# One attention-and-MLP kernel, four tables: another order, other engines for evictions and masks, other PSUM banks and turns

## The chip, the cores and the metric

The kernel runs on one core of a Trainium2 chip. The metric is the time of one execution on the device in microseconds (us); less is better. TensorE is called PE, VectorE DVE, ScalarE ACT, GpSimd POOL, and SP is the engine whose queue issues all DMAs.

## The reference, cut to what matters

```
x = A_x                                        # 1 x 2048 x 512, bf16
x = x + A(layernorm(x), A_wqkv, A_wo)          # twice, with the same weights:
x = x + B(layernorm(x), B_w1, B_b1, B_w2, B_b2)
x = x + A(layernorm(x), ...);  x = x + B(layernorm(x), ...)

def A(x, wqkv, wo):                            # 32 heads of 16, window of 256
    q, k, v = split(x @ wqkv)
    scores = q k^T * 16 ** -0.5, kept where 0 <= i - j < 256
    return (softmax(scores) v) @ wo
def B(x, w1, b1, w2, b2):                      # 512 -> 1792 -> 512
    return gelu(x @ w1 + b1) @ w2 + b2
```

## The kernel before

The 2048 rows are 16 tiles of 128, and the two repetitions give 32 tile numbers (0 to 31). Attention works on 16 blocks of two tiles. For a block, layernorm runs on DVE (statistics, L618 and L620) and POOL (the power -0.5, L630); the normalized tile xn (L640) is transposed by a DMA into xnTA (L645; the first four tiles by PE); PE makes Q and K (8 matmuls of 256 columns for two of four chunks, L666) and V (4 matmuls of 512 per tile), which ACT or DVE evict from PSUM (L609 on ACT, L607 on DVE, K always on DVE at L700). V is copied by two DMAs to Vs, shifted by half a tile (L715).

The scores come in *visits*: a block has 10 of them, numbered from 0 (block 0 and block 8, which begin a repetition, have 5). A visit is 8, 12 or 24 small matmuls of 32 rows (L767) into four PSUM banks, then two exps of 128x1024 on ACT (L774), each of which frees two banks, then one or two masks that multiply E (L795, on DVE or POOL). Two *P times V steps* per block (L819, 128 small matmuls, 64 in blocks 0 and 8) need all visits of their half; DVE and POOL transpose and normalize the result (L828, L832, L836, L842), and four matmuls per tile with Wo and a residual addition (L868) end the attention.

The MLP runs in ten jobs (0 to 9) of 2 or 4 tiles: xnTB by DMA transpose, 14 chunks of W1 (4 matmuls each, of 512 or 256 columns), gelu on ACT (6 chunks get their bias on DVE first, L891; ACT loads another table whenever it turns from exp to gelu or back), then per tile 14 matmuls with W2 and an addition on DVE (L911). W1 and W2 are both W_sb in the profile; W2's rows have gT beside it, W1's xnTB. 18 dummy matmuls (L559) on zeros fill PE where nothing else is there.

The program first builds a list of 3078 nodes, in the order of the algorithm. Every engine runs its own queue in order. What stands where is set by tables of numbers that were written beforehand: `_ORDER`, the order of all nodes, from which each engine's queue follows; `_ALT`, the nodes that run on their second engine (ACT instead of DVE for an eviction, POOL instead of DVE for a mask or a normalization, DVE instead of POOL for an epsilon addition); `_BANKS`, the PSUM bank of each allocation in that order, of eight; `_TURNS`, pairs of nodes of which the second waits for the first although it needs nothing of it. `_Plan.run` applies them, and `_Sched.op` puts in a semaphore wait wherever a node depends on another engine's node:

```
for i in _ALT:
    nodes[i]["eng"], nodes[i]["fn"] = nodes[i]["alts"][1]
for a, z in zip(_TURNS[0::2], _TURNS[1::2]):
    nodes[a]["writes"] = nodes[a]["writes"] + ["turn%d" % z]
    nodes[z]["reads"] = nodes[z]["reads"] + ["turn%d" % z]
    nodes[z]["deps"].add(a)
```

Of the kernel before, what the change touches and what calls it, by code (L numbers as in the profile page):

```python
# [19 lines left out]
class _Sched:  # L20
# [147 lines left out]
    3, 14, 4, 0, 16, 33, 1, 18, 2, 34, 20, 37, 24, 32, 56, 36, 17, 35, 57, 25, 58, 60, 19, 61, 41, 59, 22, 62, 106,  # L168
    46, 63, 30, 64, 39, 67, 65, 27, 104, 40, 68, 66, 21, 107, 29, 38, 105, 69, 15, 108, 23, 109, 49, 80, 81, 82, 54,
    113, 70, 83, 110, 114, 55, 5, 111, 6, 71, 115, 72, 112, 73, 84, 116, 13, 126, 74, 117, 42, 118, 47, 119, 152, 194,  # L170
    120, 7, 127, 48, 150, 128, 195, 129, 131, 153, 97, 151, 130, 154, 98, 196, 99, 155, 100, 85, 86, 8, 324, 101, 366,
    9, 87, 156, 368, 88, 158, 75, 103, 76, 521, 10, 90, 91, 367, 11, 102, 92, 89, 93, 12, 77, 197, 78, 94, 198, 322,
    132, 200, 133, 369, 134, 79, 143, 144, 157, 135, 199, 202, 145, 96, 146, 204, 136, 201, 95, 147, 137, 138, 139,
    325, 323, 203, 216, 140, 121, 159, 122, 326, 123, 217, 205, 124, 327, 26, 141, 125, 218, 212, 328, 207, 330, 214,
    522, 160, 206, 208, 161, 162, 163, 213, 329, 170, 43, 370, 209, 164, 171, 210, 372, 148, 172, 173, 175, 149, 176,
    174, 31, 371, 215, 374, 177, 178, 376, 211, 331, 165, 219, 166, 167, 44, 519, 168, 375, 379, 179, 142, 381, 220,
    45, 378, 520, 169, 373, 180, 380, 181, 182, 221, 183, 384, 184, 383, 337, 386, 338, 222, 339, 382, 340, 185, 223,
    385, 394, 28, 377, 224, 395, 225, 341, 226, 230, 231, 388, 396, 232, 233, 387, 398, 234, 227, 397, 400, 228, 389,
    229, 399, 306, 237, 402, 235, 187, 403, 188, 238, 332, 236, 390, 189, 239, 190, 240, 404, 347, 348, 349, 241, 350,
    191, 243, 407, 351, 523, 342, 408, 524, 343, 344, 345, 242, 401, 333, 409, 346, 412, 334, 335, 244, 414, 352, 353,  # L180
    525, 354, 50, 527, 355, 413, 359, 336, 411, 360, 51, 361, 362, 391, 192, 356, 405, 563, 415, 252, 565, 253, 259,
    416, 260, 357, 262, 254, 263, 363, 193, 261, 281, 255, 564, 410, 256, 248, 392, 249, 257, 282, 528, 245, 250, 246,
    266, 269, 247, 270, 267, 406, 526, 284, 258, 264, 285, 641, 52, 283, 417, 271, 393, 53, 268, 265, 186, 272, 418,
    273, 286, 278, 251, 279, 287, 275, 274, 276, 639, 280, 288, 544, 419, 545, 289, 546, 420, 422, 277, 567, 547, 556,
    421, 557, 307, 308, 640, 558, 642, 568, 548, 423, 643, 559, 644, 424, 425, 560, 309, 310, 645, 569, 427, 647, 428,
    311, 426, 290, 312, 313, 571, 432, 646, 314, 566, 573, 315, 433, 562, 316, 317, 318, 319, 572, 570, 320, 576, 648,
    321, 429, 577, 430, 534, 574, 539, 431, 540, 541, 578, 581, 434, 535, 542, 582, 579, 435, 529, 896, 530, 536, 537,
    543, 583, 649, 436, 650, 651, 437, 652, 538, 591, 653, 438, 531, 532, 584, 659, 593, 291, 580, 549, 533, 550, 551,
    592, 552, 440, 292, 293, 553, 294, 595, 585, 660, 597, 661, 441, 575, 295, 898, 662, 586, 596, 439, 358, 599, 587,
    296, 554, 600, 297, 298, 299, 561, 300, 301, 601, 588, 604, 663, 365, 589, 302, 303, 605, 304, 449, 487, 456, 305,  # L190
    457, 606, 897, 609, 458, 450, 611, 654, 607, 655, 590, 442, 656, 610, 657, 899, 452, 451, 453, 658, 443, 475, 613,
    463, 454, 464, 459, 444, 460, 476, 469, 461, 455, 470, 900, 484, 594, 472, 465, 901, 445, 471, 446, 466, 477, 603,
    467, 447, 462, 478, 473, 902, 479, 468, 485, 602, 664, 474, 612, 665, 480, 481, 608, 482, 486, 598, 666, 903, 448,
    904, 683, 667, 483, 503, 614, 905, 488, 364, 615, 489, 684, 490, 491, 555, 492, 685, 687, 616, 668, 493, 617, 494,
    688, 495, 496, 497, 498, 689, 686, 691, 618, 499, 500, 693, 501, 624, 625, 502, 626, 627, 692, 696, 628, 669, 670,
    698, 671, 695, 631, 672, 916, 690, 917, 697, 632, 673, 701, 918, 919, 702, 619, 699, 620, 920, 621, 703, 711, 700,
    622, 504, 505, 623, 713, 704, 506, 507, 508, 629, 509, 712, 715, 510, 630, 511, 1016, 633, 716, 676, 634, 677,
    1018, 678, 679, 717, 719, 705, 512, 637, 513, 514, 694, 721, 515, 714, 706, 1019, 1017, 718, 720, 680, 1020, 638,
    1021, 724, 707, 723, 516, 681, 726, 517, 921, 722, 922, 675, 923, 708, 924, 725, 518, 729, 925, 933, 730, 934,
    935, 936, 731, 727, 906, 728, 940, 1024, 907, 941, 908, 733, 909, 732, 942, 709, 734, 710, 937, 910, 1022, 944,  # L200
    735, 943, 926, 946, 927, 928, 929, 911, 945, 1023, 736, 912, 948, 737, 930, 947, 738, 1025, 913, 949, 914, 739,
    939, 740, 915, 741, 742, 950, 635, 953, 743, 744, 745, 955, 951, 746, 749, 747, 636, 954, 748, 958, 952, 1036,
    1037, 751, 1038, 959, 1039, 750, 752, 1040, 753, 960, 968, 754, 969, 757, 1026, 1027, 962, 1028, 1029, 957, 970,
    755, 972, 1030, 758, 974, 956, 976, 961, 977, 756, 963, 971, 674, 973, 682, 964, 978, 981, 932, 975, 982, 786,
    965, 787, 979, 1273, 788, 789, 983, 986, 1274, 790, 781, 980, 782, 988, 770, 985, 771, 772, 773, 987, 984, 1060,
    783, 784, 1061, 764, 989, 765, 775, 785, 776, 990, 1062, 777, 766, 774, 778, 1064, 779, 767, 966, 1066, 991, 768,
    1065, 1068, 992, 792, 1070, 793, 794, 795, 812, 1063, 1069, 827, 993, 828, 967, 829, 830, 802, 1072, 1275, 803,
    813, 814, 832, 815, 1276, 797, 798, 796, 822, 817, 1277, 831, 818, 1278, 799, 800, 780, 1031, 823, 1279, 996,
    1032, 994, 997, 801, 824, 825, 816, 759, 819, 1280, 1281, 820, 791, 760, 995, 848, 804, 805, 761, 821, 998, 807,
    808, 826, 1067, 762, 809, 864, 810, 806, 763, 999, 1001, 811, 1002, 1000, 1003, 1071, 1004, 769, 1033, 1034, 1005,  # L210
    1073, 833, 1006, 834, 835, 1008, 836, 837, 838, 1007, 839, 1009, 1074, 840, 1010, 1035, 849, 1011, 850, 851, 1075,
    852, 1014, 1078, 853, 1080, 854, 1076, 855, 1395, 856, 1077, 857, 858, 1079, 1088, 1012, 841, 842, 1089, 1081,
    859, 860, 861, 1082, 843, 1090, 1013, 844, 845, 846, 862, 847, 1092, 1015, 1041, 1093, 1042, 863, 880, 1043, 931,
    1044, 1083, 1094, 938, 1045, 1096, 1282, 1084, 881, 1097, 882, 883, 884, 865, 1396, 866, 1393, 1098, 867, 1101,
    1394, 1095, 868, 1103, 869, 1397, 1099, 870, 871, 1091, 872, 1398, 873, 1102, 1106, 885, 1399, 886, 1108, 1085,
    887, 888, 1086, 889, 890, 1107, 1317, 1100, 1104, 874, 875, 1319, 891, 1109, 892, 893, 894, 1318, 1321, 895, 876,
    877, 1105, 878, 1087, 1322, 1298, 1299, 1110, 879, 1300, 1301, 1323, 1293, 1294, 1302, 1295, 1296, 1325, 1324,
    1297, 1111, 1327, 1326, 1330, 1112, 1332, 1329, 1288, 1331, 1113, 1335, 1401, 1114, 1289, 1290, 1337, 1291, 1121,
    1328, 1115, 1122, 1336, 1345, 1292, 1123, 1124, 1320, 1116, 1347, 1117, 1334, 1125, 1118, 1338, 1119, 1346, 1349,
    1128, 1283, 1284, 1120, 1285, 1350, 1286, 1333, 1129, 1303, 1126, 1304, 1351, 1353, 1127, 1305, 1287, 1130, 1306,  # L220
    1131, 1354, 1339, 1046, 1047, 1048, 1134, 1049, 1355, 1352, 1358, 1132, 1050, 1360, 1340, 1357, 1135, 1307, 1356,
    1359, 1363, 1341, 1133, 1310, 1364, 1361, 1311, 1051, 1312, 1053, 1054, 1365, 1342, 1437, 1362, 1348, 1055, 1056,
    1439, 1313, 1366, 1136, 1137, 1367, 1057, 1314, 1368, 1343, 1438, 1400, 1650, 1441, 1440, 1369, 1402, 1138, 1442,
    1139, 1158, 1058, 1159, 1160, 1140, 1161, 1443, 1059, 1445, 1162, 1141, 1052, 1142, 1447, 1444, 1143, 1344, 1144,
# [758 lines left out]
```

## Time and profile before

| | |
|---|---|
| median of 3 runs | 439.81 us (438.87 to 440.06) |
| the profiled execution | 440.44 us; its span from first to last instruction 438.9 us |
| TensorE's granted clock | 0.998 of full speed |
| busy: PE, ACT, DVE, POOL | 412.5, 386.6, 335.6, 209.1 us |
| DMA | 23.51 MB, 161 DMAs issued by SP |

In the rows of the profile an engine's busy time is the union of its instructions, so matmuls that overlap count once. A row of the timeline merges neighbours of one kind: where it starts, how long it lasts, what it is, how many, and in brackets how long the engine idled ahead of it and what ended that.

### The profile page before, as it was taken

What the parts mean: (1) busy time and instruction counts of PE and PEld (TensorE: products, weight loads), DVE (VectorE), ACT (ScalarE), POOL (GpSimd) and SP (SyncE); (2) the same over time, 40 slices, a digit from 0 to 9 for tenths busy, and PEclk for the clock granted to TensorE, in tenths of its full rate; (3) what the DMA queues carried; (4) which work ended last, traced back from release to release, by engine and by line L of the source; (5) the groups of instructions that cost most, each with busy time, mean ns of one, the idle gap of its engine ahead of it and who ended that gap; (6) DMA issues with size and microseconds to landing.
All of it is one profiled execution on the core that took longest, in us unless ns stands there. A gap on an engine that the chain in (4) does not pass through costs nothing.

```text
span 438.9 us, 16863 instructions
## 1 busy us (share of the span) xinstructions
PE 412.5 (94%) x7497; PEld 227.9 (52%) x7571; DVE 335.6 (76%) x635; ACT 386.6 (88%) x458; POOL 209.1 (48%) x233
## 2 busy tenths in 40 slices
PE   8989999998699988999999999999999999999995
PEld 4555756554444544454454455454564554444662
DVE  6999878689867788976899687878877586655841
ACT  3999988999999899999999999999889989899442
POOL 4675263372555366731566344442443645635140
PEclk9999999999999999999999999999999999999999
DMA  7782812102300303212040111201322013003030
GB/s 234 216 210 39 221 32 52 38 21 40 58 3 13 52 4 46 32 34 44 10 94 2 25 27 28 52 1 33 43 55 50 1 31 82 7 0 76 3 108 25
DMA packets 49060, 23.51 MB, mean 54 GB/s; under 512 B 34268, under 2 KB 48988, under 8 KB 48988
## 3 DMA queue, kind: packets, MB, share of 16 engines
q1 hardware_dynamic: 48988, 22.43, 23.2%
q8 instruction: 60, 0.98, 1.0%
q14 instruction: 12, 0.10, 0.1%
HBM read 8.00 MB, written 2.10 MB: 23 GB/s over the span
## 4 chain that ended last, share of the span: by engine, by line
PE 76%; ACT 10%; DVE 6%; DMA 3%; issue 3%; POOL 1%; SPq 1%; POOLq 0%; DVEq 0%
PE ps L666 59%; ACT E L774 9%; PE ps L767 9%; PE ps L819 7%; DVE OD L828 1%; DVE KT L700 1%; POOL E L795 1%; DMA xnTA<-xn 1%; DMA xnTB<-xn 1%; DVE X L911 1%; DVE stat L618 1%; SPq L645 1%; ACT Va L609 0%; DMA X<-in_A_x_dram 0%; DVE E L795 0%
## 5 line engine op out<-in xcount | busy, mean ns | idle before, releaser
L774 ACT ACTIVATE E<-ps 128x1024 bf16<-128x1024 f32 x300 | 284.0, 1038 | 21.7 <-PE ps L767 20.2
L795 POOL TENSOR_TENSOR E<-E,mask 128x512 bf16<-128x512 bf16 (+2 forms) x112 | 121.6, 1097 | 107.7 <-ACT E L774 43.8
L666 PE MATMUL ps<-W_sb,gT 128*128 128x512 bf16 x415 | 106.5, 380 | 3.2 <-issue 2.5
L666 PE MATMUL ps<-xnTB,W_sb 128*128 128x512 bf16 (+1 forms) x542 | 105.5, 335 | 3.6 <-issue 1.6
L666 PEld LDWEIGHTS ps<-xnTB,W_sb 128*128 128x128 bf16 x560 | 52.0, 98 | 43.9 <-issue 4.3
L666 PE MATMUL ps<-xnTA,Wqkv_sb 128*128 128x256 bf16 x512 | 70.6, 273 | 2.2 <-DVE OD L828 1.1
L767 PE MATMUL ps<-QT,KT 32*128 32x128 bf16 (+3 forms) x1920 | 60.6, 231 | 4.9 <-ACT E L774 2.0
L795 DVE TENSOR_TENSOR E<-E,mask 128x512 bf16<-128x512 bf16 (+2 forms) x124 | 51.2, 438 | 14.1 <-ACT E L774 6.8
L666 PEld LDWEIGHTS ps<-W_sb,gT 128*128 128x128 bf16 x448 | 39.4, 98 | 43.1 <-issue 3.4
L828 DVE STREAM_TRANSPOSE OD<-ps 128x1024 f32<-128x1024 f32 x32 | 40.0, 1249 | 23.7 <-PE ps L819 23.5
L666 PEld LDWEIGHTS ps<-xnTA,Wqkv_sb 128*128 128x128 bf16 x512 | 46.3, 98 | 22.5 <-issue 3.2
L767 PEld LDWEIGHTS ps<-QT,KT 32*128 32x128 bf16 x1920 | 28.5, 92 | 51.3 <-ACT E L774 31.0
L899 ACT ACTIVATE gT<-ps,b1T 128x512 bf16<-128x512 f32 (+1 forms) x80 | 43.7, 606 | 10.1 <-PE ps L666 10.0
L907 POOL TENSOR_TENSOR Xb<-X,b2all 128x512 f32<-128x512 bf16 x32 | 36.8, 1152 | 20.4 <-DVE X L911 11.5
L618 DVE BATCH_NORM_STATS2 stat<-X 128x6 f32<-128x512 bf16 x64 | 43.3, 684 | 2.5 <-DMA X<-in_A_x_dram 1.7
L819 PE MATMUL ps<-E,Va 64*17 64x192 bf16 (+3 forms) x1920 | 39.9, 230 | 3.0 <-ACT E L774 1.3
L700 DVE TENSOR_TENSOR KT<-ps,parmask 128x1024 bf16<-128x1024 f32 x32 | 38.6, 1211 | 5.3 <-PE ps L666 5.1
L891 DVE TENSOR_SCALAR gT<-ps,b1T 128x512 bf16<-128x512 f32 (+1 forms) x60 | 36.8, 631 | 6.3 <-PE ps L666 5.9
L836 POOL TENSOR_TENSOR Nb<-OD,Rc 128x512 bf16<-128x512 f32 x18 | 19.0, 1056 | 42.9 <-DVE Rc L832 28.6
L819 PE MATMUL ps<-E,Vs 64*17 64x128 bf16 (+3 forms) x1920 | 39.2, 230 | 0.0
L630 POOL TENSOR_TENSOR rstd<-rstd,mhalf 128x2 f32<-128x2 f32 (+1 forms) x33 | 24.3, 736 | 28.9 <-DVE rstd L624 27.2
L911 DVE TENSOR_TENSOR X<-Xb,ps 128x512 bf16<-128x512 f32 x32 | 21.6, 682 | 19.2 <-PE ps L666 19.0
(49 smaller groups left out, 362.3 us busy)
## 6 DMA issues: line engine op xcount, KB each, us to landing
Vs<-Va SPq DMA_DIRECT2D x64, 68.0 KB, 2.9
W_sb<-in_B_w_dram SPq DMA_DIRECT2D x4, 512.0 KB, 4.6
out_dram<-X SPq DMA_DIRECT2D x16, 128.0 KB, 2.0
X<-in_A_x_dram SPq DMA_DIRECT2D x3, 512.0 KB, 6.6
Wqkv_sb<-in_A_wqkv_dram SPq DMA_DIRECT2D x4, 256.0 KB, 7.3
W_sb<-in_B_w_dram SPq DMA_DIRECT2D x1, 768.0 KB
W_sb<-in_B_w_dram SPq DMA_DIRECT2D x2, 384.0 KB, 5.2
Wqkv_sb<-in_A_wqkv_dram SPq DMA_DIRECT2D x1, 512.0 KB, 6.9
```

What stands on the lines that cost most here:

```text
L618: add("dve", lambda e, B, t=t, k6=k6: e.bn_stats(stat6[:, k6, :], X[:, t, :]), reads=["X%d" % t], writes=["st%d" % k6], key="bs%d" % (k + j))
L666: r = e.matmul(ps[:, B[g][0], cols], lhsT, rhs, start=st, stop=sp)
L700: add("dve", lambda e, B, g=g, i=i: e.tensor_tensor(out=KT[:, kb, 2 * i : 2 * i + 2].rearrange("p c m a q -> p a (c m) q"), in0=ps[:, B[g] ...
L767: x = e.matmul(ps[:, bk[r], o : o + n], KT[rows, kb, c, m].rearrange("p a q -> p (a q)"), QT[rows, c, q : q + n], start=True, stop=True)
L774: add("act", lambda e, B, g_=g_, gi=gi: e.activation(E[:, 2 * gi : 2 * gi + 2, e0 : e0 + 512], ps[:, B[g_][0] : B[g_][0] + 2, :], AF.Exp, ...
L795: fn = lambda e, B: e.tensor_tensor(out=Ew, in0=Ew, in1=Mw, op=ALU.mult)
L819: x = e.matmul(ps[32 * r : 32 * r + VW, B[g][par], c % 2 * 2 * P + lo : c % 2 * 2 * P + hi], V[rows, (2 * b + m // 2) % VR, c * HC + 2 * r ...
L828: add("dve", lambda e, B: e.transpose(OD[:, s].rearrange("p a c q -> p (a c q)"), ps[:, B[g][0] : B[g][0] + 2, :]), reads=["ps:" + g], wri ...
L891: add("dve", lambda e, B, g=g, fc=fc: e.tensor_scalar(out=gT[:, fc, c0 : c0 + M], in0=ps[:, B[g][0], 0:M], scalar1=b1T[:, fc : fc + 1], sc ...
L899: add("act", lambda e, B, g=g, fc=fc: e.activation(gT[:, fc, c0 : c0 + M], ps[:, B[g][0], 0:M], AF.Gelu_apprx_tanh, bias=b1T[:, fc : fc + ...
L907: add("pool", lambda e, B, t=t, xs=xs: e.tensor_tensor(out=Xb[:, xs, :], in0=X[:, t, :], in1=b2all[:], op=ALU.add), reads=["X%d" % t, "b2a ...
L911: add("dve", lambda e, B, g=g, t=t, xs=xs: e.tensor_tensor(out=X[:, t, :], in0=Xb[:, xs, :], in1=ps[:, B[g][0], :], op=ALU.add), reads=["X ...
```

## The change

The four tables are replaced; no line of the program besides them differs, and the 3078 nodes are the same. The tables' numbers tell a reader nothing, so the first lines of two stand for them. The new tables are two lines shorter, so line 666 before is line 664 after.

```
 _ORDER = [
-    3, 14, 4, 0, 16, 33, 1, 18, 2, 34, 20, 37, 24, 32, 56, 36, 17, 35, 57, 25, 58, 60, 19, 61, 41, 59, 22, 62, 106,
...
 _ALT = [
-    62, 66, 69, 74, 94, 101, 108, 115, 120, 184, 191, 197, 201, 206, 210, 215, 219, 356, 363, 369, 373, 377, 378, 383,
...
```

ACT has 440 nodes before and 435 after, DVE 635 and 647, POOL 229 and 222; PE keeps 1613 and SP 161. `_ALT` names 171 nodes before and 163 after, `_TURNS` has 182 pairs before and 166 after. A node's place in PE's queue moves by 10.5 places on average, at most 94.

Three places show what moves. The first is on PE, in attention block 4, from its visit 3 to its visit 7. L767 rows are visits (QT and KT are Q and K transposed), the others what PE does between them. Before:

```order
L767 MATMUL ps<-QT,KT 128x192 x8
L767 MATMUL ps<-QT,KT 128x128 x4
L666 MATMUL ps<-Wo_sb,OT 128x512 x4
L767 MATMUL ps<-QT,KT 128x128 x8
L767 MATMUL ps<-QT,KT 128x64 x16
L666 MATMUL ps<-xnTA,Wqkv_sb 128x256 x8
L767 MATMUL ps<-QT,KT 128x256 x8
L666 MATMUL ps<-xnTA,Wqkv_sb 128x256 x8
L767 MATMUL ps<-QT,KT 128x256 x8
L767 MATMUL ps<-QT,KT 128x192 x8
L767 MATMUL ps<-QT,KT 128x128 x4
```

and after, where L767 has become L765:

```order
L765 MATMUL ps<-QT,KT 128x192 x8
L765 MATMUL ps<-QT,KT 128x128 x4
L664 MATMUL ps<-Wo_sb,OT 128x512 x5
L765 MATMUL ps<-QT,KT 128x128 x8
L765 MATMUL ps<-QT,KT 128x64 x16
L664 MATMUL ps<-Wo_sb,OT 128x512 x3
L664 MATMUL ps<-Wqkv_sb,xnTA 128x512 x4
L765 MATMUL ps<-QT,KT 128x256 x8
L664 MATMUL ps<-xnTA,Wqkv_sb 128x256 x8
L765 MATMUL ps<-QT,KT 128x256 x8
L765 MATMUL ps<-QT,KT 128x192 x8
L765 MATMUL ps<-QT,KT 128x128 x4
```

The last two rows of each piece are visit 7. Before, the gaps hold four matmuls with Wo, eight for K and eight for Q, and nothing ahead of visit 7; after, eight with Wo, four for V and eight for K, and again nothing ahead of visit 7.

The second place is on PE in block 6, from visit 3 on. The piece of before ends with visit 6, the one of after just ahead of it. Before:

```order
L767 MATMUL ps<-QT,KT 128x192 x8
L767 MATMUL ps<-QT,KT 128x128 x4
L666 MATMUL ps<-xnTA,Wqkv_sb 128x256 x2
L767 MATMUL ps<-QT,KT 128x128 x8
L767 MATMUL ps<-QT,KT 128x64 x16
L666 MATMUL ps<-xnTA,Wqkv_sb 128x256 x6
L666 MATMUL ps<-Wo_sb,OT 128x512 x2
L767 MATMUL ps<-QT,KT 128x256 x8
L666 MATMUL ps<-Wo_sb,OT 128x512 x6
L767 MATMUL ps<-QT,KT 128x256 x8
```

and after:

```order
L765 MATMUL ps<-QT,KT 128x192 x8
L765 MATMUL ps<-QT,KT 128x128 x4
L664 MATMUL ps<-xnTA,Wqkv_sb 128x256 x8
L664 MATMUL ps<-W_sb,gT 128x512 x4
L765 MATMUL ps<-QT,KT 128x128 x8
L765 MATMUL ps<-QT,KT 128x64 x16
L664 MATMUL ps<-W_sb,gT 128x512
L664 MATMUL ps<-Wo_sb,OT 128x512 x4
L664 MATMUL ps<-W_sb,gT 128x512
L765 MATMUL ps<-QT,KT 128x256 x8
L664 MATMUL ps<-W_sb,gT 128x512 x2
L664 MATMUL ps<-Wo_sb,OT 128x512 x4
```

The W_sb,gT rows are tile 7's matmuls with W2. Before, all of them are done ahead of visit 1 of this block; after, eight of the fourteen stand in these gaps, and Q's eight are no longer split by a visit.

The third place is SP's queue, near the start. Before, from the load of Wo to the DMA transpose of tile 7 (the last row):

```order
L586 DMA Wo_sb<-in_A_wo_dram 128x4x512
L715 DMA Vs<-Va 64x544 x2
L645 DMA_TRANSPOSE xnTA<-xn 128x4x128
L715 DMA Vs<-Va 64x544 x2
L645 DMA_TRANSPOSE xnTA<-xn 128x4x128
L715 DMA Vs<-Va 64x544
L645 DMA_TRANSPOSE xnTA<-xn 128x4x128
L588 DMA W_sb<-in_B_w_dram 128x4x768
L715 DMA Vs<-Va 64x544 x2
L645 DMA_TRANSPOSE xnTA<-xn 128x4x128
```

and after, from a load of W2 (128x4x512 at L595) to the first transposes into xnTB; tile 7's transpose is the second of the pair ahead of Wo:

```order
L595 DMA W_sb<-in_B_w_dram 128x4x512
L713 DMA Vs<-Va 64x544 x2
L586 DMA W_sb<-in_B_w_dram 128x4x512
L643 DMA_TRANSPOSE xnTA<-xn 128x4x128 x2
L584 DMA Wo_sb<-in_A_wo_dram 128x4x512
L565 DMA X<-in_A_x_dram 128x4x512
L713 DMA Vs<-Va 64x544 x2
L595 DMA W_sb<-in_B_w_dram 128x4x512
L643 DMA_TRANSPOSE xnTB<-xn 128x4x128 x2
```

Wo is loaded behind tile 7's transpose, where it was loaded ahead of all transposes. The two loads of W2's first eight chunks (the first row of this piece and the one ahead of xnTB) stood before next to each other, behind the first two transposes into xnTB.

At the program's end, PE's queue after has job 9's 56 matmuls with W1 in one piece, then tile 31's 14 with W2, then tile 30's 14; before, the matmuls of both tiles are mixed with each other and with job 9's.

394 rows, old and new, of tables (_ALT, _BANKS, _ORDER, _TURNS) are left out of this document.

## The prediction

> **What bounds the kernel now.** I read the page's engine shares and chain first, then the busy time by stretches of 20 us, then the timeline where TensorE falls short. The page:
>
> ```profile
> PE 412.5 (94%) x7497; PEld 227.9 (52%) x7571; DVE 335.6 (76%) x635; ACT 386.6 (88%) x458; POOL 209.1 (48%) x233
> PE 76%; ACT 10%; DVE 6%; DMA 3%; issue 3%; POOL 1%; SPq 1%; POOLq 0%; DVEq 0%
> ```
>
> TensorE (PE) is the bound: 412.5 of 438.9 us busy and 76% of the chain. ScalarE (ACT) is close behind with 386.6. The change gives PE no less to do, so only PE's idle time, 26 us, can be won or lost. The stretches say where it lies (span, then busy time of PE, weight loads, DVE, ACT, POOL, granted clock):
>
> ```profile
> 20.00:40.00 20.00, 17.58 (x446) 11.31 (x444) 18.89 (x33) 18.91 (x22) 15.16 (x18) 1.00 0.55 132
> 40.00:60.00 20.00, 18.87 (x298) 12.02 (x300) 15.92 (x32) 18.30 (x27) 8.10 (x10) 1.00 0.68 152
> 80.00:100.00 20.00, 18.80 (x447) 9.76 (x450) 16.25 (x30) 19.46 (x23) 11.04 (x13) 1.00 0.16 33
> 100.00:120.00 20.00, 15.06 (x434) 8.75 (x434) 17.62 (x34) 19.59 (x23) 8.67 (x10) 1.00 0.31 53
> 160.00:180.00 20.00, 17.97 (x438) 9.12 (x443) 18.24 (x36) 18.94 (x22) 11.69 (x13) 1.00 0.34 43
> 240.00:260.00 20.00, 19.73 (x378) 9.96 (x383) 14.95 (x30) 19.52 (x24) 8.22 (x11) 1.00 0.14 28
> 340.00:360.00 20.00, 19.53 (x416) 10.74 (x419) 13.65 (x24) 18.27 (x23) 9.97 (x11) 1.00 0.04 9
> ```
>
> From 240 us on PE idles 0.3 to 0.5 us in 20: nothing is to be won there, only lost. Before 180 us it loses 2.4, 1.1, 1.2, 4.9 and 2.0 us in the five stretches shown. In the worst one, 100 to 120 us, ACT is busy 19.59 of 20: there PE waits for ACT.
>
> **The prices.** Timeline rows of PE (start, length, line, operation, count; L666 are full-width matmuls, L767 a visit of scores, L819 the P times V step):
>
> ```profile
> 97.34 0.40 PE L767 MATMUL ps<-QT,KT 32*128 32x192 bf16 x12
> 98.12 1.04 PE L666 MATMUL ps<-xnTA,Wqkv_sb 128*128 128x256 bf16 x8
> 99.09 0.41 PE L767 MATMUL ps<-QT,KT 32*128 32x128 bf16 x24
> 118.69 0.81 PE L666 MATMUL ps<-xnTB,W_sb 128*128 128x512 bf16 x3 [0.82 <-ACT E L774]
> 119.43 0.70 PE L767 MATMUL ps<-QT,KT 32*128 32x128 bf16 x24
> 121.46 0.40 PE L767 MATMUL ps<-QT,KT 32*128 32x256 bf16 x8
> 121.79 1.90 PE L666 MATMUL ps<-xnTB,W_sb 128*128 128x512 bf16 x8
> 124.66 0.24 PE L819 MATMUL ps<-E,Va 64*17 64x64 bf16 x8
> 125.90 0.40 PE L767 MATMUL ps<-QT,KT 32*128 32x192 bf16 x12
> ```
>
> A 512-column matmul costs (1.90 - 0.81) / 5 = 0.218 us, I take 0.216. A visit costs 121.79 - 121.46 = 0.33. Three matmuls from 118.69 end their issue at 119.34 and the visit starts at 119.43: a change from full-width work to a visit costs 0.10. Eight 256-column matmuls take 99.09 - 98.12 - 0.10 = 0.87, so 0.11 each. A P times V step costs 125.90 - 124.66 = 1.24. For ACT (a row of the chain, and two rows of groups):
>
> ```profile
> 107.22 12.94 ACT E L774 x14
> L609 ACT ACTIVATE Va<-ps 128x512 bf16<-128x512 f32 x17 | 10.5, 615 | 0.8 <-PE ps L666 0.8
> L607 DVE CAST Va<-ps 128x512 bf16<-128x512 f32 x15 | 10.2, 687 | 1.6 <-PE ps L666 1.3
> ```
>
> One exp costs 12.94 / 14 = 0.924 us, an eviction 0.6. A visit feeds two exps (1.85 us of ACT) and takes 0.43 of PE: PE needs 1.42 us of other work, some 6.5 matmuls of 512 columns, between two visits, or it runs ahead of ACT until the PSUM banks are full, and waits.
>
> **The change, part by part.** PE gets the same instructions, ACT the same exps and gelus and as many table loads, so nothing is removed. Five evictions go from ACT to DVE: 5 x 0.615 = 3.1 us less on ACT and 5 x 0.687 = 3.4 us more on DVE, which has 103 us free. Of 236 masks, 56 go from POOL to DVE and 54 the other way. The rest is order.
>
> *First stage, blocks 3 to 5 (97 to 121 us).* I count the order. From visit 8 of block 3 (97.34) to visit 0 of block 5 (121.46) before issues 12 visits, 28 matmuls of 512 and 40 of 256 columns, 2 P times V steps and 10 changes: 3.96 + 6.05 + 4.40 + 2.48 + 1.00 = 17.9 us. ACT gets 24 exps and 3 evictions: 22.2 + 1.8 = 24.0. The stage took 24.1: ACT's time, and PE lost 6.2. After puts 38 instead of 28 matmuls of 512 columns there, 20.0 us (the first order excerpt shows three gaps between visits of it: 4 and 16, then 12 and 8 matmuls of 512 and 256 columns). But an excess of ACT's work over PE's can also build up over a longer piece: the worst one that I find runs from visit 1 of block 3 to visit 9 of block 4, with 36 exps and 2 evictions (34.5 us) against 18 visits, 60 and 52 matmuls, 3 steps and 15 changes (29.8 us): 4.7. The loss goes from 6.2 to 4.7, **1.5 us gained**. Bounds: 0, if ACT comes to the stage with more left to do than before; 2.8, if only the first piece counts (24 exps and 2 evictions, 23.4, against 20.0: 3.4 left of 6.2).
>
> *Second stage, blocks 6 and 7 (157 to 172 us).*
>
> ```profile
> 157.20 0.40 PE L767 MATMUL ps<-QT,KT 32*128 32x192 bf16 x12
> 172.06 0.40 PE L767 MATMUL ps<-QT,KT 32*128 32x256 bf16 x8 [0.15 <-ACT E L774]
> 173.58 0.60 PE L666 MATMUL ps<-xnTB,W_sb 128*128 128x512 bf16 x2 [0.36 <-DMA xnTB<-xn]
> 169.36 4.17 DMA xnTB<-xn
> ```
>
> Before has 21 matmuls of 512 and 16 of 256 columns, 8 visits, 2 steps, 6 changes there: 4.5 + 1.8 + 2.6 + 2.5 + 0.6 = 12.0 us; it took 14.9, so PE lost 2.9. ACT's 16 exps and an eviction are 15.4. After holds back eight matmuls of tile 7's W2 step for this place (the second order excerpt), and the largest excess I count in blocks 6 and 7 is 1.1 us (visit 9 to visit 1: 4 exps, 3.7, against 2 visits, 8 matmuls and 2 changes, 2.6). **1.8 gained**, bounds 0 (the wait only moves) and 2.9 (none is left). The wait for the transpose into xnTB that follows (0.36) I leave as it is: on SP the same two transposes stand before that job.
>
> *The SP queue.* Rows of the chain, of SP, of the DMA groups and of PE:
>
> ```profile
> 47.91 4.19 DMA xnTA<-xn
> 26.15 1.21 SPq L645 DMA_TRANSPOSE xnTA<-xn  x1
> Wo_sb<-in_A_wo_dram SPq DMA_DIRECT2D x1, 512.0 KB, 7.4
> W_sb<-in_B_w_dram SPq DMA_DIRECT2D x4, 512.0 KB, 4.6
> 32.93 1.25 PE L666 MATMUL ps<-Wo_sb,OT 128*128 128x512 bf16 x5 [0.20 <-ACT E L774]
> ```
>
> Near 48 us a transpose into xnTA is in flight for 4.19 us behind two weight loads, and the chain runs through it. After issues the two 512 KB loads of W2 ahead of the xnTB transposes that SP waits for (third excerpt), so only the two smaller ones still stand around the xnTA transposes: I credit **0.5**, of 0 to 1.0 (PE idled 1.1 from 40 to 60). Against that Wo's load is moved behind tile 7's transpose, which ended its issue at 26.15 + 1.21 = 27.4. Issued then, it lands 4.6 later, at 32.0, or with Wo's own 7.4 at 34.8; its first user starts at 32.93. I debit **0.5**, of 0 to 1.9. At the start, Wq's first half goes behind a 512 KB load of X, one transposed tile's eviction goes from ACT to DVE, and the three dummy matmuls that stood among the first scores go to the front: 0, of -0.5 to +0.5, an eviction's length either way.
>
> *The tail.*
>
> ```profile
> 433.88 1.34 DVE L911 TENSOR_TENSOR X<-Xb,ps 128x512 bf16<-128x512 f32 x2 [6.51 <-PE ps L666]
> ```
>
> Tiles 30 and 31 end together before: two additions, 1.34 us, then the last store. After runs tile 31's 14 matmuls, then tile 30's, so one addition lies under matmuls: **0.6 gained**, half of 1.34, of 0 to 0.7.
>
> *The late part, 180 to 420 us.* The evictions, masks and turns are all reassigned, but PE idles at most 0.5 in 20 us in the rows shown, so no gain; 0, to a loss of 2.
>
> **Sum:** -1.5 - 1.8 - 0.5 + 0.5 - 0.6 = -3.9 us. The profiled execution took 440.44 (span 438.9), so 436.5 for one like it. The median of the runs shown is 439.81, 0.6 lower; the forecast on that scale is **435.9**.
>
> **The rivals.** *The stalls nearly vanish.* The five stretches quoted idle 11.7 us in 100; at the 0.4 of the late ones 2.0 would be left, so 9.7 less, and 0.6 of the tail. For it: both slices hold more PE work than before. Against it: ACT still has more work than PE in the first stage. A gain of 7 to 10, about 431.3. Chance 0.14.
>
> *ScalarE sets the time whatever PE's order is.* 19.59 of 20 busy: work that PE now does inside the stage is missing ahead of it, and the wait only moves. Left are the tail's 0.6 and SP's 0.5 less 0.5: 439.2, no change that can be told. Against it: ACT is busy 18.91 and 18.30 in the two stretches from 20 to 60 and 19.46 from 80 to 100, so there is room to start earlier. Chance 0.10.
>
> *Slower: masks late in the blocks after 180 us.* Rows of groups:
>
> ```profile
> L795 POOL TENSOR_TENSOR E<-E,mask 128x512 bf16<-128x512 bf16 x59 | 67.8, 1154 | 38.4 <-DVE Nb L836 12.3 <-ACT E L774 10.6 <-DVE E L795 9.7
> L795 DVE TENSOR_TENSOR E<-E,mask 128x512 bf16<-128x512 bf16 x57 | 23.3, 414 | 5.1 <-POOL E L795 2.8 <-ACT E L774 1.6 <-POOL Xb L907 0.6
> ```
>
> 110 masks change engine, 54 of them to POOL, where one takes 0.74 us longer. A P times V step waits for its last mask, and all scores behind it wait in PE's queue. Some 18 steps lie after 180 us. If 9 of them wait 0.74, 6.7 us are lost against 3.9 gained: 442.6; it decides from 7 on (5.2, the gain and the bound of 1.3). For it: there is no idle time there to hide it. Against it: between a step and the last visit that it needs, before has 2.3 us of PE work or more by my count and after 2.9, and after's eight closest steps have their last masks on DVE. Chance 0.09. The Trainium skill (Advanced Engine Details and Errata, Mode Summary) says that VectorE's second SBUF port is shared with GpSimd and that the two block each other in the two-port modes; no row here shows a mask by itself and beside the other engine, so it changes no price; were it to bind here, the time would be this rival's.
>
> *Slower: Wo much too late.*
>
> ```profile
> 1.24 3.70 PE L559 MATMUL ps<-gT 128*128 128x512 bf16 x10 [1.24 <-DVE gT L557]
> ```
>
> If SP is held up by 3 us more ahead of Wo (landing at 37.8), PE stands still for 4.9 us at 33. The first ten dummies of the run took 3.70 us, 0.37 each against 0.216: if PE starts as slowly after such a pause, 1.5 us go as well. 6.4 lost where 0.5 was counted: 441.8. It decides from a landing at 37.1 on (4.2 of pause and 1.5, the 4.4 gained elsewhere and 1.3). Chance 0.05. The Trainium skill (TensorE: Matmul & The Clock Gate, What's actually happening) says that after an idle window of about 3.4 us the clock is halved until PE has been busy as long; the granted clock is 1.00 in every stretch quoted, where no pause is that long.
>
> **How the numbers follow.** A measurement of this kernel can tell about 0.3% (1.3 us) from no change. The forecast's case, a gain of 1.3 to 7, has 0.62; with the first rival faster has 0.76. Same has the second rival's 0.10, slower the last two with 0.14. The terms' worst ends (0 + 0 + 0 - 1.9 + 0 - 0.5 - 2) give 4.4 lost, the best ones 2.8 + 2.9 + 1.0 + 0.7 + 0.5 = 7.9 gained. The range goes from 430.7 (9.1 gained, most of the first rival) to 441.0 (1.2 lost, since not all bad ends come together); it leaves out most of the two slower cases (0.14) and a little of the first rival.
>
> **What would show it.** In the profile after, PE's busy time in 100 to 120 should rise from 15.06 to about 16.5, and in 160 to 180 from 17.97 to over 19; the visit that began at 172.06 should begin 2 to 4 us earlier; the last pair of additions should no longer be one piece of 1.34. The first Wo matmul should start by 33.5. I am wrong if the first stage loses 6 us again, if PE idles over 1 us in 20 after 200 us, or if P times V waits for POOL's masks there.

## The result

The kernel after takes 443.65 us (median of 20 runs, 439.51 to 446.68) against 439.44 for the kernel before on the same chip (20 runs, 438.64 to 440.77): a ratio of 1.0088, 95% interval 1.0074 to 1.0102. It is slower by 0.9%, where 435.9 was forecast. The ratio leaves out two runs of after that took over 1.5% more than its fastest one, 446.68 us and the profiled one, 446.44. So the trace of after (span 444.5) shows one of its slowest executions, 2.8 us above the median, and sums over its stops stand for that execution; the profiled one of before took 440.44, span 438.9.

The page of after (busy time; then the queue by which PE's code comes, with packets, MB and share; then the chain):

```profile
PE 416.2 (94%) x7507; PEld 230.1 (52%) x7571; DVE 340.7 (77%) x647; ACT 384.7 (87%) x453; POOL 200.5 (45%) x226
q8 instruction: 59, 0.97, 1.0%
PE 81%; DVE 6%; ACT 4%; issue 4%; DMA 3%; SPq 1%; POOL 1%; DVEq 0%
```

The stretches of 20 us of after, with the columns of those before:

```profile
40.00:60.00 20.00, 18.56 (x312) 12.47 (x315) 17.05 (x33) 18.08 (x26) 10.50 (x11) 1.00 0.50 97
60.00:80.00 20.00, 16.50 (x309) 10.76 (x305) 12.80 (x25) 14.81 (x16) 10.64 (x12) 0.91 0.16 35
100.00:120.00 20.00, 16.99 (x485) 9.86 (x471) 18.19 (x37) 19.83 (x23) 8.19 (x11) 1.00 0.24 47
160.00:180.00 20.00, 18.53 (x567) 10.30 (x568) 19.19 (x36) 18.73 (x21) 11.99 (x13) 1.00 0.19 40
200.00:220.00 20.00, 18.80 (x378) 9.88 (x382) 16.14 (x32) 19.15 (x23) 8.02 (x7) 1.00 0.10 22
280.00:300.00 20.00, 18.61 (x268) 9.56 (x269) 12.81 (x24) 18.78 (x24) 12.00 (x12) 1.00 0.20 29
380.00:400.00 20.00, 18.25 (x232) 8.52 (x234) 12.43 (x23) 16.68 (x20) 6.41 (x6) 1.00 0.02 6
```

The two stages that the prediction speaks of did get better: PE is busy 16.99 of 20 where it was 15.06 (about 16.5 was forecast), and 18.53 where it was 17.97 (over 19 was forecast). The visit that began at 172.06, forecast 2 to 4 us earlier, begins at 174.99, 2.9 later. But there are new holes: 3.5 us at 60 to 80, where ScalarE and VectorE run dry together with PE and the clock drops to 0.91, and 1.2 to 1.8 us in three late stretches. The timeline shows what they are. PEld's rows are weight loads, the bracket holds the idle time ahead of a row and what ended it; L817 is a P times V step, L664 a matmul with Wo, L765 the visit just named, L909 the additions at the end:

```profile
33.56 0.59 PE L664 MATMUL ps<-Wo_sb,OT 128*128 128x512 bf16 x2
...
73.01 0.10 PEld L817 LDWEIGHTS ps<-E,Va 64*17 64x17 bf16 x4 [3.19 <-issue]
...
174.99 0.40 PE L765 MATMUL ps<-QT,KT 32*128 32x256 bf16 x8 [0.30 <-DVE OD L826]
...
391.58 0.09 PEld L817 LDWEIGHTS ps<-E,Va 64*17 64x17 bf16 x3 [1.58 <-issue]
...
438.68 0.69 DVE L909 TENSOR_TENSOR X<-Xb,ps 128x512 bf16<-128x512 f32 x1 [4.79 <-PE ps L664]
441.70 0.69 DVE L909 TENSOR_TENSOR X<-Xb,ps 128x512 bf16<-128x512 f32 x1 [2.34 <-PE ps L664]
```

PE stops for 3.19 and 1.58 us *inside* a P times V step, on "issue", that is on nothing that the profile shows. A step is one node; its semaphores are waited for ahead of its first matmul, so no mask, bank or load can stop it behind its 100th pair, as at 73.01.

Counting PE's instructions gives the answer. A matmul is two instructions (weight load and matmul); a wait that doesn't fit on one is another. The step at 73.01 stops at instruction 2241, the one at 391.58 at 14017: both are 193 modulo 256. Every stop of this kind in after, and in before, lies at 193 or 194 modulo 256. PE's 15,289 instructions in after are 59.7 times 256, and the instruction queue moved 59 packets of 16,384 bytes each, which is 64 bytes for each of 256 instructions. So PE's code comes in pages of 256 instructions, and PE stands where a page isn't there yet. For the stops, from the packets' own times:

| PE enters a page | the next page's packet starts | ends | PE goes on |
|---|---|---|---|
| 36.96 (after) | 38.61 | 39.54 | 40.97 |
| 66.64 (after) | 70.67 | 71.69 | 73.01 |
| 295.98 (after) | 296.96 | 298.41 | 299.72 |
| 387.27 (after) | 388.96 | 390.18 | 391.58 |
| 102.85 (before) | 104.43 | 105.39 | 106.79 |

The packet for the next page starts 1.1 us (median in after; 1.0 in before) after PE has entered the page before and takes 0.9 to 1.7 us; where PE waited for it, PE goes on 1.2 to 1.6 us behind its end: some 3.5 us in all. A page full of 512-column matmuls lasts some 28 us (128 x 0.216), but a P times V step is a page by itself (128 pairs), and it lasts 1.25. Where most of such a step falls into one page, the next one can be late. Some packets also start late: ten of after's start 2.5 to 4.3 us after their page was entered. The longest stop is such a case, for its packet started 4.0 us after 66.64; had it started after 1.1, some 0.3 us would be left of the 3.2 (an estimate from these times). Before has three late pages that cost 1.5 us together (106.8, 119.8, 381.5); after has twelve, eleven that cost something to speak of, 10.0 us together (the longest 3.16 at 73.0). In after the granted clock is 0.5 for 3.41 us from 72.7, where the longest pause ends, and again from 120.4.

### The profile page after: what moved, and what is told of

It is laid out like the page before. It is cut to its first block, busy times and chain, and to the rows that moved or that the text cites. A ratio compares the mean times of both kernels' runs of the same rounds, so it can differ in the third digit from the quotient of the medians.

```text
span 444.5 us, 16849 instructions
## 1 busy us (share of the span) xinstructions
PE 416.2 (94%) x7507; PEld 230.1 (52%) x7571; DVE 340.7 (77%) x647; ACT 384.7 (87%) x453; POOL 200.5 (45%) x226
## 4 chain that ended last, share of the span: by engine, by line
PE 81%; DVE 6%; ACT 4%; issue 4%; DMA 3%; SPq 1%; POOL 1%; DVEq 0%
PE ps L664 63%; PE ps L765 10%; PE ps L817 8%; ACT E L772 4%; DMA Wqkv_sb<-in_A_wqkv_dram 2%; DMA xnTB<-xn 1%; DVE OD L826 1%; DVE E L793 1%; DVE KT L698 1%; SPq L570 1%; DVE Nb L834 0%; DVE OT L840 0%; DVE xn L638 0%; POOL E L793 0%; DVE Va L605 0%
## 5 line engine op out<-in xcount | busy, mean ns | idle before, releaser
L793 POOL TENSOR_TENSOR E<-E,mask 128x512 bf16<-128x512 bf16 (+2 forms) x110 | 118.7, 1091 | 126.0 <-ACT E L772 59.5
L664 PE MATMUL ps<-W_sb,gT 128*128 128x512 bf16 x416 | 106.5, 381 | 3.2 <-issue 2.1
L664 PE MATMUL ps<-xnTB,W_sb 128*128 128x512 bf16 (+1 forms) x544 | 102.6, 337 | 3.3 <-issue 2.0
L664 PEld LDWEIGHTS ps<-xnTB,W_sb 128*128 128x128 bf16 x560 | 52.7, 98 | 42.8 <-issue 2.1
L664 PE MATMUL ps<-xnTA,Wqkv_sb 128*128 128x256 bf16 x512 | 68.2, 276 | 1.1 <-ACT E L772 0.5
L765 PE MATMUL ps<-QT,KT 32*128 32x128 bf16 (+3 forms) x1920 | 61.9, 233 | 5.9 <-ACT E L772 2.2
L664 PEld LDWEIGHTS ps<-W_sb,gT 128*128 128x128 bf16 x448 | 39.4, 98 | 44.3 <-issue 5.4
L765 PEld LDWEIGHTS ps<-QT,KT 32*128 32x128 bf16 x1920 | 28.9, 93 | 55.7 <-ACT E L772 31.5
L664 PEld LDWEIGHTS ps<-xnTA,Wqkv_sb 128*128 128x128 bf16 x512 | 47.1, 98 | 18.0 <-issue 2.7
L817 PE MATMUL ps<-E,Va 64*17 64x192 bf16 (+3 forms) x1920 | 40.4, 230 | 6.6 <-issue 4.4
L817 PE MATMUL ps<-E,Vs 64*17 64x128 bf16 (+3 forms) x1920 | 39.8, 231 | 0.0
L628 POOL TENSOR_TENSOR rstd<-rstd,mhalf 128x2 f32<-128x2 f32 (+1 forms) x33 | 22.9, 693 | 36.6 <-DVE rstd L622 24.9
L817 PEld LDWEIGHTS ps<-E,Va 64*17 64x17 bf16 x1920 | 27.6, 84 | 17.1 <-issue 12.1
L909 DVE TENSOR_TENSOR X<-Xb,ps 128x512 bf16<-128x512 f32 x32 | 21.6, 679 | 18.6 <-PE ps L664 15.9
```

The lines of the kernel that those rows point to most:

```text
L628: add("pool", lambda e, B, j=j, n=n: e.tensor_tensor(out=rstd[:, k + j : k + j + n], in0=rstd[:, k + j : k + j + n], in1=mhalf[:, 0:n], op ...
L664: r = e.matmul(ps[:, B[g][0], cols], lhsT, rhs, start=st, stop=sp)
L765: x = e.matmul(ps[:, bk[r], o : o + n], KT[rows, kb, c, m].rearrange("p a q -> p (a q)"), QT[rows, c, q : q + n], start=True, stop=True)
L793: fn = lambda e, B: e.tensor_tensor(out=Ew, in0=Ew, in1=Mw, op=ALU.mult)
L817: x = e.matmul(ps[32 * r : 32 * r + VW, B[g][par], c % 2 * 2 * P + lo : c % 2 * 2 * P + hi], V[rows, (2 * b + m // 2) % VR, c * HC + 2 * r ...
```

## The experiments

The theory: the pages of PE's code, which no table of the kernel knows of, gave back more than the order won. Its rivals: masks that come late (the prediction's), loads at the start, the clock alone. The clock alone falls short, for one run of after took 444.74 us with a granted clock of 1.0. And the waits of after's trace name no mask on POOL ahead of a P times V step, where before's name five, 1.8 us together.

**One shift of all of before's code.** 84 increments of a semaphore that nobody waits for, strewn over PE's first 30 us, move all later code by 84 places; a second kernel has the same 84 in PE's last 26 us, where two pages still end, both without a stop.

```
+_PADS = {1: 2, 2: 2, 3: 2, 4: 2, 5: 2, ...}
...
+                        for _ in range(_pads.get(j, 0)):
+                            e.sem_inc(self.pad_sem, 1)
                         cl(e)
```

> The kernel before, with 84 semaphore increments that nobody waits for strewn over the first 30 us of PE's queue. Nothing else moves, but every later instruction of PE stands 84 places later in PE's stream. Theory of code pages: PE's instructions come 256 at a time, in packets of 16,384 bytes; in both traces a packet starts about 1.05 us after PE has entered the page before and can be used 1.35 us after its end, some 3.5 us in all, and a page that PE uses up sooner leaves PE standing. Before has four such late pages (1.5 us), after twelve (10.0 us), always at the same place modulo 256. With the ends of the pages moved by 84 I work out some 20 us of waits for before's own stream: 455 to 465 us, with most of the waits inside P times V steps or visits. Theory of late masks and theory of the clock alone: nothing that they speak of is changed, so 439 to 441 us (84 increments take 84 x 0.051 = 4.3 us of PE's sequencer, most of it under matmuls).

> The kernel before, with the same 84 increments, strewn over the last 26 us of PE's queue, behind the last end of a page. The price of the increments without the shift. Theory of code pages: within 1 us of the kernel before, 439 to 441 us. If the increments themselves cost what the shifted kernel loses, it is as slow as that one, 455 or more.

Measured: 469.88 us with the shift (ratio 1.0673, 1.0635 to 1.0711), 439.71 without (0.9998, 0.9978 to 1.0018). The order, the engines and the waits are those of before, and it loses 30 us. The timeline of PEld in the shifted kernel (L778 a visit, L830 a P times V step):

```profile
244.62 0.10 PEld L778 LDWEIGHTS ps<-QT,KT 32*128 32x128 bf16 x1 [2.55 <-issue]
...
404.23 0.11 PEld L830 LDWEIGHTS ps<-E,Va 64*17 64x17 bf16 x9 [2.21 <-issue]
```

Sixteen stops of over 0.2 us, 25 us together by the idle time of the weight loads, again at 193 or 194 modulo 256 and each 1.2 to 1.6 us behind the end of its page's packet (one, of 2.2 us at 265, the profile puts down to a wait for ScalarE). That is more than the 20 us that I had worked out, and the time lies above the 455 to 465 that I gave. The rest of the 30 goes with six windows of 3.41 us at half clock and what they and the stops push back; how they share it I can't tell. Before stood well by its place in the pages, and nothing in its tables says so.

**The page rate by itself.** Eight more P times V steps behind everything else:

```
+        nd = next(n for n in PL.nodes if n["key"] == "pv15_1")
+        for _ in range(8):
+            S_.op("pe", lambda e, fn=nd["fn"]: fn(e, B), reads=phys(nd["reads"]), writes=phys(nd["writes"]))
```

> The kernel before, with block 15's second P times V step repeated eight times behind everything else in PE's queue (1024 more pairs of weight load and matmul; the results are not used). Eight pages of code in a row with no other work. One such step takes 1.25 us in the trace of before. Theory of code pages: each of the eight takes the time of a page, 3.4 us, some 27 us in all, and PE stands inside each step. If PE's code comes fast enough: 8 x 1.25 = 10 us.

Measured: 464.24 us in a single run, 24.5 more than before's median. PE's rows in the added steps:

```profile
444.07 0.23 PE L819 MATMUL ps<-E,Vs 64*17 64x64 bf16 x4 [1.62 <-issue]
447.56 0.23 PE L819 MATMUL ps<-E,Vs 64*17 64x64 bf16 x4 [1.17 <-issue]
451.04 0.23 PE L819 MATMUL ps<-E,Vs 64*17 64x64 bf16 x4 [1.16 <-issue]
454.51 0.23 PE L819 MATMUL ps<-E,Vs 64*17 64x64 bf16 x4 [1.15 <-issue]
```

PE stops once in every page, and the stops follow each other by 3.47 to 3.49 us here (3.46 to 3.85 over all seven). From 441.35 on the granted clock is 0.5 and a step takes 2.1 us instead of 1.25, but the distance stays: in this run it is the pages that set the pace, 256 instructions in some 3.5 us, and not PE's work.

**Padding after, first try: a miss.** 288 such increments in after, where they take the ends of pages out of the dense stretches.

> The kernel after, with 288 semaphore increments that nobody waits for, put in PE's queue where they move the ends of its code pages off the dense stretches (pages 1, 2, 5, 10, 15, 16, 44, 45 and 53). Order, engines, banks and turns stay. Theory of code pages: nearly all of the 10.0 us that PE stood at the ends of pages goes, and with the long stops the dips of the clock: 433 to 437 us, faster than both kernels, with no gap over 0.4 us inside a P times V step. Theory of late masks, and of late loads at the start: the masks and the loads stand where they stood, so 443 us or more. Theory of the clock alone (the granted clock falls for a reason other than these stops): 442 to 444 us, with a granted clock below 0.997 as before.

Measured: 460.6 us (1.0474, 1.0445 to 1.0502). One stop of over 0.2 us is left at the end of a page (1.7), so the pages did what was asked. But increments behind each other follow by 0.151 us, not by the 0.051 of their rows, and PE starved behind them (L678 matmuls with Wq or Wk, between increments):

```profile
115.34 0.38 PE L678 MATMUL ps<-xnTA,Wqkv_sb 128*128 128x256 bf16 x2 [0.53 <-issue]
116.30 0.38 PE L678 MATMUL ps<-xnTA,Wqkv_sb 128*128 128x256 bf16 x2 [0.58 <-issue]
117.96 0.37 PE L678 MATMUL ps<-xnTA,Wqkv_sb 128*128 128x256 bf16 x1 [1.28 <-issue]
```

The granted clock was 0.5 for 27.3 us of this run, 17.1 of them from 117.4 on, right behind these rows. The run says nothing on the theory; padding has to cost PE nothing.

**Padding that costs nothing: split matmuls.** A 512-column matmul in two halves is two instructions more and as much work.

```
+                        if _LEFT[0] and cols == slice(0, 512):
+                            _LEFT[0] -= 1
+                            e.matmul(ps[:, B[g][0], 0:256], lhsT, rhs[:, 0:256], start=st, stop=False, ...)
+                            r = e.matmul(ps[:, B[g][0], 256:512], lhsT, rhs[:, 256:512], start=False, stop=sp, ...)
+                            continue
```

> The kernel after, with 99 of its 512-column matmuls written as two of 256 columns (0.11 us each, against 0.216) and 16 of the dummy matmuls at the start written as four of 128 columns: 294 more instructions in PE's stream, which move the ends of the code pages off the dense stretches, as the increments did, but hardly any time on PE. Order, engines, banks and turns stay, and every element is computed in the same order. Theory of code pages: the 10.0 us of waits at the ends of pages go, and the dips of the clock that follow the long ones (1.5 us): 432 to 437 us; no wait at the end of a page over 0.7 us; granted clock 0.998 or more. Theory of late masks or loads: 443 us or more, since nothing of them is changed. Theory that the increments' kernel was slow because of waits that moved elsewhere: 440 or more.

> The kernel before, with 137 of its 512-column matmuls written as two of 256 columns, so that its own four late pages (1.5 us) are moved off the dense stretches too. Theory of code pages: 437.5 to 439.5 us, a gain of at most 1.5 us: before's order stood well already. What the split of matmuls costs or gains by itself is bounded by the same run: 137 x 0.002 = 0.3 us. If splits help for another reason than the pages, the gain is as large as in the kernel after.

Measured: after split 437.93 us (0.9952, 0.9933 to 0.9970), before split 439.33 (0.9980, 0.9966 to 0.9994). With its order, engines, banks and turns kept and only the places of its pages moved, the kernel after turns from 0.9% slower than before to 0.5% faster, while such splits in before bring 0.2%. That rules out masks, loads and the engines of evictions as the cause of the loss: they are all still there. No window at half clock is left in its profile, and three late pages are, 2.0 us together. One of them, 1.45 us at 38, is longer than the 0.7 that I allowed, and the time lies 0.9 above my range.

**Two refinements that brought nothing.** The split places chosen anew, and two moves at the start:

```
+for _x in (26, 28, 25, 17):   # four dummies behind tile 1's transpose
+    _move(_x, 68)
+_move(35, 36)                 # Wq's first half behind Wk's
```

> The kernel after, split as in after_split but with the places chosen anew from that kernel's trace, where three late pages were left (waits of 1.44, 0.39 and 0.18 us at 37.7, 72.7 and 103.2 us): 95 matmuls with W1, W2, Wv or Wo in halves, 16 dummies in quarters. Theory of code pages: 436 to 438 us, up to 1.5 us below after_split, with at most one wait over 0.5 us at the end of a page. If what is left against the sum of my terms is the start of the order and not the pages, no change against after_split (437.5 to 438.5).

> after_split2 with two changes of the order at the start: the load of Wq's first half goes ahead of the 512 KB load of X again, as before, and four of the dummy matmuls go behind the first two transposed tiles, as before. At W = 10 us of PE work the trace of after stands 1.1 us behind that of before. If these two moves are why, 435 to 437 us, 0.5 to 1.2 us below after_split2, and the first matmuls with Wq wait for no load (0.47 to 0.73 us in the kernels after). If the start is absorbed by ScalarE's work behind it, the same as after_split2 within 0.4 us.

Measured: 438.40 us (0.9971, 0.9954 to 0.9988) and 438.53 (0.9973, 0.9954 to 0.9991), no different from after_split or from each other. The late page at 38 us stayed in both, with waits of 1.45 and 1.79 us, and the start was not made earlier: where PE has had 10 us of work it stands 1.1 us behind before in after, 1.2 and 1.5 in these. What costs it that 1 us stays open.

**The page at 38 us.** In the split kernels three loads of 512 KB (Wo, four tiles of X, four of W2's fourteen chunks) are in flight up to 37 us; PE enters a page at 33.7 to 34.0, and the next one's packet starts at 36.7 to 37.4, as the loads end. So one load was moved:

```
+_ORDER.remove(54)                              # load of X, tiles 12 to 15
+_ORDER.insert(_ORDER.index(526) + 1, 54)       # behind tile 8's transpose
```

> after_split with one load moved in SP's queue: the 512 KB load of tiles 12 to 15 of X goes from its place right behind Wo's load to behind tile 8's transpose (its first use is at 68 us). In the kernels after, three 512 KB loads are in flight from 31 to 37 us, and the code page that PE asks for at 33.7 is fetched only when they are done, at 36.7 to 37.0 (elsewhere a page is fetched about 1 us after PE has entered the one before); PE waits 1.4 to 1.6 us for it at 37.7. Theory that bulk loads hold up the code page: the loads end by 35.5, the page is fetched 1.4 us earlier, the wait falls below 0.4 us, and 0.5 to 1.5 us are gained: 436.5 to 437.4. Theory that the page is late for another reason (its place among PE's instructions): the wait stays at 1.4 and the time at 437.9.

Measured: 436.65 us (0.9925, 0.9906 to 0.9943). The packet starts 0.55 us after its page is entered, at 35.2, and PE doesn't wait. This is the fastest kernel of the study, 0.75% faster than before, though its interval still overlaps that of after_split. Its stretches:

```profile
60.00:80.00 20.00, 19.78 (x374) 13.53 (x376) 15.24 (x31) 19.05 (x27) 14.28 (x16) 1.00 0.17 33
100.00:120.00 20.00, 17.25 (x448) 11.79 (x449) 17.09 (x32) 18.48 (x21) 8.69 (x10) 0.91 0.26 54
160.00:180.00 20.00, 18.85 (x449) 10.17 (x451) 19.22 (x37) 18.75 (x21) 12.39 (x13) 1.00 0.30 55
280.00:300.00 20.00, 19.68 (x402) 11.12 (x404) 14.53 (x30) 19.59 (x24) 10.77 (x13) 1.00 0.04 10
380.00:400.00 20.00, 19.42 (x420) 9.73 (x423) 11.08 (x21) 18.80 (x23) 9.28 (x10) 1.00 0.11 28
```

60 to 80, 280 to 300 and 380 to 400 are full again; the waits for ScalarE at 100 to 120 remain, as predicted. They cost clock as well: from 114.9 on it is 0.5 for 3.41 us, which the page ends have no part in and which makes PE look busier in that row.

**The second stage undone, and the masks' engines given back.** From after_split3, once with tile 7's W2 matmuls 6 to 13 ahead of visit 2 of block 6, once with the 110 masks on before's engines:

```
+_Y = [887, 888, 889, 890, 891, 892, 893, 894]
+_ORDER = [x for x in _ORDER if x not in _Y]
+_i = _ORDER.index(886) + 1
+_ORDER[_i:_i] = _Y
```

```
+_ALT = sorted((set(_ALT) - {...54 masks...}) | {...56 masks...})
```

> after_split3 with the second stage undone: the eight matmuls of tile 7's W2 step that the order after holds back for block 6's gaps (six to thirteen of its fourteen) stand ahead of visit 2 of block 6 again, so that they no longer lie between the visits that ScalarE is behind on. My term for this stage: 1.8 us lost again (0 to 2.9), 437.5 to 439.5. If the wait only moves with the matmuls, as one bound of the term had it: no change, within 0.5 us of after_split3. The ends of the code pages move by 16 instructions in this stretch alone; a late page there would show in the trace and is counted apart.

> after_split3 with the 110 masks that the change gave another engine given back to the engine of before (56 to POOL, 54 to VectorE); order, banks and turns stay those of after. Theory of late masks (my rival for slower): the assignment of after costs up to 0.74 us for each P times V step that waits, so this kernel is 1 to 6 us faster than after_split3. Theory of code pages: masks were not what cost the time; within 1 us of after_split3, or slower, since the order of after was chosen with its own masks' engines.

Measured: 438.38 us (0.9972, 0.9957 to 0.9988) without the second stage's move, 1.7 above after_split3 and clear of its interval. Its stretch there, and PE at 17.01 where it was 18.85:

```profile
160.00:180.00 20.00, 17.01 (x424) 8.55 (x414) 19.02 (x36) 18.69 (x21) 11.69 (x13) 1.00 0.24 51
```

With before's engines for the masks 457.52 us (1.0399, 1.0370 to 1.0428): 21 us slower, the other way than my rival had it. So after's order needs its own engines for the masks. One reason shows in the groups (here after_split3m; a 512-wide mask on DVE took 414 ns in before and 415 in after_split3) and the timeline:

```profile
L836 DVE TENSOR_TENSOR E<-E,mask 128x512 bf16<-128x512 bf16 x57 | 33.6, 594 | 5.0 <-POOL Xb L948 3.3 <-ACT E L815 1.2 <-POOL E L836 0.5
```

```profile
157.07 3.41 POOL L836 TENSOR_TENSOR E<-E,mask 128x768 bf16<-128x768 bf16 x2
157.12 3.64 DVE L836 TENSOR_TENSOR E<-E,mask 128x512 bf16<-128x512 bf16 x2
```

In before and in after_split3 no mask on DVE runs beside a mask on POOL, 0 of 124 and 0 of 126. Here 34 do, and take 1.00 us on average against 0.44 for the others: a mask on DVE that starts during one on POOL mostly ends 0.28 to 0.42 us behind it. How much of the 21 us comes of this, and how much of masks that the order has too late or too early, is not shown.

## Why the prediction was wrong, step by step

To compare stages I price PE's work with the prediction's prices, sum it up along PE's queue, and take the sum from the time at which PE gets there. What is left is what PE has lost so far (us; "u" is the kernel with the second stage undone):

| PE's work done | before | after | after_split3 | u |
|---|---|---|---|---|
| 50 | 7.35 | 9.04 | 8.21 | 8.52 |
| 90 | 8.27 | 15.12 | 9.81 | 10.74 |
| 110 | 14.50 | 19.35 | 14.48 | 14.37 |
| 140 | 14.73 | 19.26 | 14.38 | 14.17 |
| 160 | 18.15 | 20.62 | 15.39 | 17.36 |
| 180 | 18.54 | 21.21 | 15.51 | 17.47 |
| 410 | 18.60 | 25.78 | 15.97 | 18.15 |
| last matmul to the end | 4.98 | 3.40 | 3.41 | 3.43 |

*What bounds the kernel* was read wrongly in one point: "only PE's idle time can be won or lost" holds, but I asked only which engine or load PE would wait for. The code itself was no candidate, and the sum has no term for it. That is the step that failed. In the profiled executions after's late pages cost 10.0 - 1.5 = 8.5 us more than before's, against the 3.9 that the order was to win; and with the page ends moved the loss is gone.

*First stage* (work 90 to 110): a loss of 6.2 was to become 4.7, and it is 4.7 in after_split3 (4.2 in after). The direction is right; that the number fits is in part luck. After_split3 has its window at half clock there, and u, with the same order in this piece and no such window, loses 3.6, close to the 3.4 of the shorter piece that was my bound. Which piece sets the loss the runs don't tell.

*Second stage* (140 to 160): a loss of 2.9 was to become 1.1. Over this somewhat longer piece it goes from 3.4 to 1.0 (1.4 in after), and with the move undone it is 3.2 again. The visit after it begins 1.9 us earlier than in before once the page ends are moved (170.20 in after_split3). The forecast gain of 1.8 is 2.0 to 2.4 by the traces, and 1.7 to 2.1 by the times of that experiment (the medians; 0.9972 - 0.9925 of 440).

*SP's queue and the start* were to cancel. They don't: at 50 us of work after is 1.7 us behind before, after_split3 0.9. Wo's first matmul started at 33.56, against "by 33.5", so Wo was not late. What I had missed is that the moved loads, together, hold up a page of code (1.5 us of the wait at 38 in after_split, shown by moving one load), and that the start loses 1.1 us in the first 10, which I had bounded at 0.5.

*The tail* was to gain 0.6, of 0 to 0.7. From the last matmul to the end it is 5.0 before and 3.4 after: 1.6 gained. I had priced the addition that goes under matmuls, not the store behind it.

*The late part* was to change nothing, and "PE idles over 1 us in 20 after 200 us" was named as the sign that I am wrong. It does, by up to 1.75 (380 to 400), but mostly on pages: with their ends moved, the loss from 180 on is 0.5 instead of 4.6; before has 0.1.

The two slower rivals didn't happen: no P times V step of after waits for a mask on POOL, and Wo landed in time. Slower came by a third way. The sum over the order itself was close: after_split3's span is 434.7 against 438.9, 4.2 less, of which some 1.1 are before's own late pages that it avoids. I had 3.9. That the two agree is in part luck: the start loses 0.9 where it was to lose nothing, and the tail wins 1.0 more than its term.

The Trainium skill bears on two of these. Its page "Runtime: NRT & Kernel Launch" (Instruction fetch mechanics) says that code is refilled in blocks of 16 KiB, 256 instructions, and that crossing into the next one is "mostly hidden". The block's size agrees with the packets here; "mostly hidden" doesn't where PE runs short matmuls: 10.0 us in after, some 25 in the shifted kernel. What the prediction cites from the Trainium skill, "Advanced Engine Details and Errata" (Mode Summary), on the port that VectorE shares with GpSimd, now has a row here: 34 masks at 1.00 us against 0.44. The prediction priced a mask given to POOL at 0.74 us; where two masks meet, VectorE's takes longer as well, and in the kernels before and after none meet.

## What to carry over

A reordered instruction stream moves its code pages too. Count PE's instructions (two per matmul, 256 to a page here) and compare the time that each page lasts with the 3.5 us that the next one needs: a burst of 128 short matmuls in one page costs some 2.2 us (3.5 less its own 1.25), more where the packet starts late, and splitting some hundred wide matmuls elsewhere moved it at almost no cost here. A wait on "issue" in the middle of one step, with the engines behind PE running dry, is how it looks in a profile. And when a search yields an order a per cent slower than its own sums say, shift the code by a few dozen instructions before blaming the order.

## What the runs showed of the hardware

- PE's code comes 256 instructions at a time; a page can be used some 3.5 us after the one before it was entered, and seven dense pages in a row took 3.46 to 3.85 us each.
- Bulk loads in flight hold up a page's packet: it started 2.8 to 3.3 us after its page was entered, behind three loads of 512 KB, and 0.55 us with one of them moved. They are not the only cause: in after the packets behind the entries at 73.01 and 391.58 started 3.2 and 3.1 us late with no other transfer in flight. Why stays open.
- After pauses of PE the granted clock is 0.5 in windows of 3.41 us, which lie on one grid: those of after, from 72.65 and 120.44, are 14 windows of 3.413 us apart. In the 3.41 us ahead of them PE was busy for 0.8 and 1.4 us. "TensorE: Matmul & The Clock Gate" (What's actually happening) in the Trainium skill gives about 3.4 us as the idle window; the length of the windows agrees, but the windows ahead were not wholly idle here.
- Semaphore increments on PE follow each other by 0.151 us though each row shows 0.051.
- A mask on VectorE beside one on GpSimd is delayed: 1.00 us on average against 0.44.
